# Recurrent attention with two feed-forward stages on one core: the bonus product and its transpose at other places of the unit

## The chip, the cores and the metric

The kernel runs on one core of one Trainium2 chip. The metric is the device time of one execution in microseconds (us); the time before is the median of three runs.

## The reference, cut to what matters

Three stages follow one another. The first is a linear recurrence per batch and head, with a 48 x 48 state, over 768 steps:

```
for t in range(S):
    cur   = outer(u * k[t], v[t])                  # the bonus of the present step
    y[t]  = r[t] @ (state + cur)
    state = w[t][:, None] * state + outer(k[t], v[t])
```

The second is a feed-forward layer on all 3072 tokens, `h = x @ w_in`, `g = h * tanh(softplus(h))`, `x = g @ w_out`. The third routes each token greedily to one of 8 experts of 384 places each, and applies `relu(x @ w1[e]) @ w2[e]`.

## The kernel before, in words

The recurrence is cut into 24 *units*: two groups of 12 consecutive time chunks, each of two sequences' chunk of 64 steps for all 8 heads. The units of a group depend on each other through the state `S`. A unit consists of ten steps, each a small function:

- `att0` (scan of the decays `E`, and `rk` = r * k), `att_inv`, `att1` and `att1b` (scaling of r and k with the decays and their inverses; ScalarE does Ln and Exp, VectorE the rest),
- `bon1` (L423: u times `rk`, the bonus of every step, 16 matmuls into a `Y` buffer, then `bT` by ScalarE) and `bon2` (L429: one transpose of `bT` into another `Y` buffer, then `bt` by ScalarE and L434, which spreads it into the diagonal of `Dt`),
- `att_A` (scores and the state's part, into `A`; then L467 puts the scores into `Dt`), `att_K` (transposes of k into `Y`, moved out as `kn`),
- `att_S` (L494: the new part of the state, into two `Y` buffers; L501 and L503 add and scale on VectorE), and `att4` (L516: the output matmuls; then `xg`, the input of the second stage, by ScalarE and L523; for every second unit six small DMAs move some rows of `xg`, L529).

The pool that `Y` comes from has two buffers, taken in turn by `bon1`, `bon2`, `att_K` and twice by `att_S`. An engine works its instructions off in the order in which they were written.

The second stage runs along with the recurrence. Its tokens are in 12 groups of 256 (two units each); a group has 8 *slots*, a unit therefore four. In each slot stands one chunk of the first product (`mm1`, L611, 18 matmuls into `Hp`, two buffers; ScalarE evicts each twice, as `es` and `hs`) and a share of the second product (`mm2_part`, L659). Per four slots ScalarE does Arctan and two Sin (L621, L631), and Sigmoid, Sin and Ln with Exp each need a table load when their turn comes.

The order of all this is a list of events with a time in slots each, sorted by time; nothing else orders it. The table `CFG` gives the times; a step of unit n stands at 4n - 13 plus the number in `CFG['u']`, which `CFG['un']` may replace for one unit:

```
for nm, o in {**CFG["u"], **CFG["un"].get(n, {})}.items():
    at(4 * n - 13 + o, steps[nm], n)
...
at(t + CFG["mm1"], mm1, t // NS, t % NS)
at(t + CFG["mm2"], mm2, t)
```

`mm1` stands at 0.7 of a slot, `mm2` at 0.275 of the next, `att_S` of a unit at 7.29 and `att4` at 7.3, which is 3.29 and 3.3 in the count of the unit after it. The third stage is not touched.

Of the kernel before, what the change touches and what calls it, by code (L numbers as in the profile page):

```python
# [25 lines left out]
 'ogT': [7.4, 8.45, 9.9, 10.25, 10.95, 11.85, 12.55, 12.75],  # L26
 'ogM': [8.15, 9.35, 10.2, 10.9, 11.35, 11.95, 12.75, 13.95],
 'u': {'att0': -0.5,
       'bon1': 2.57,
       'bon2': 3.5,  # L30
       'r1': 2.7,
       'k1': 3.175,
       'K': 4.91,
# [53 lines left out]
            'k1': 3.2},  # L87
        5: {'y': 7.46,
            'att0': -1.5,
            'bon1': 3.27,  # L90
            'bon2': 5.25,
            'inv': 3.67,
            'r1': 3.7,
            'k1': 4.3,
# [5 lines left out]
            'A1': 6.67,  # L100
            'S': 7.4,
            'att0': 0.0,
            'bon1': 2.87,
            'bon2': 3.85,
            'inv': 3.27,
            'r1': 3.3,
            'k1': 3.9},
        7: {'bon1': 1.37,
            'att0': -0.5,
            'bon2': 4.85,  # L110
            'inv': 2.77,
            'r1': 2.8,
            'k1': 3.4,
# [1 line left out]
            'A1': 5.87,  # L115
            'S': 7.29,
            'y': 7.3},
        20: {'A1': 5.62, 'bon1': 2.57},
        22: {'att0': -0.6, 'bon1': 1.77, 'bon2': 2.45, 'K': 4.46},
        23: {'K': 3.81, 'A1': 6.0, 'y': 7.1}},  # L120
 'rate': [(9, 0), (80, 194), (82, 200), (85, 216), (89, 218), (93, 234), (99, 258)],
 'close_cv': 15.0,
 'close_att': 86.65,
# [1212 lines left out]
```

## Time and profile before

| | |
|---|---|
| median of three runs | 914.36 us (911.02 to 915.53) |
| the profiled execution | 911.8 us |
| its span | 910.1 us |
| TensorE busy | 780.0 us, 86% |
| VectorE busy | 533.2 us, 59% |
| ScalarE busy | 511.5 us, 56% |
| GpSimd busy | 67.0 us, 7% |
| mean granted TensorE clock | 0.933 |

The times of the profile are those of one execution, counted from the start of its span. An engine's busy time is the time in which it executes instructions; the granted clock is the share of TensorE's full clock. In a timeline a row that ends in brackets tells how long the engine stood idle before it and what released it. PE is TensorE, DVE VectorE, ACT ScalarE.

### The profile page before, as it was taken

The page shows a single profiled execution, that of the slowest core. Times are in us where ns is not written, and L with a number is a line of the kernel's source. Part 1 is how long each engine was busy: PE and PEld are TensorE (multiplying, and loading weights), DVE is VectorE, ACT ScalarE, POOL GpSimd, SP SyncE. Part 2 cuts the span into 40 slices and gives each one's busy share as a digit, 9 for nine tenths or more (in the row PEclk, how much of TensorE's full clock was granted, in tenths as well). Part 3 has the DMA queues.
Part 4 walks back from the last instruction along what each step waited for, and adds up shares of the span by engine and source line. Part 5 has one row for each costly group of instructions (what it writes and reads, how often), then busy time and mean ns, then how long its engine had stood idle before and what let it go on. Part 6 is the DMA issues. An engine that isn't in the chain of part 4 may idle for free. (4 is left out here: it accounts for less than half of the span.)

```text
span 910.1 us, 20168 instructions
## 1 busy us (share of the span) xinstructions
PE 780.0 (86%) x8819; PEld 530.5 (58%) x8819; DVE 533.2 (59%) x933; ACT 511.5 (56%) x728; POOL 67.0 (7%) x104
## 2 busy tenths in 40 slices
PE   6874879788897888888879799999987999999997
PEld 3553656566675555556557577655545655555564
DVE  6699856756556555666555633467774455555420
ACT  3357979876776666666676757711002445445421
POOL 2000000000000000000000000100002122223311
PEclk9796999998999889988889999999996999999999
DMA  7950503211212212212202000040042455544300
GB/s 274 268 148 5 174 10 68 54 40 45 49 38 48 49 39 44 47 34 52 45 10 49 15 10 14 15 160 19 19 157 55 165 183 183 182 166 152 117 27 26
DMA packets 22220, 74.12 MB, mean 81 GB/s; under 512 B 4496, under 2 KB 13072, under 8 KB 20080
## 3 DMA queue, kind: packets, MB, share of 16 engines
q1 hardware_dynamic: 19056, 63.35, 23.9%
q0 software_dynamic: 3072, 9.44, 3.3%
q8 instruction: 71, 1.16, 0.6%
q14 instruction: 21, 0.17, 0.1%
HBM read 62.15 MB, written 9.44 MB: 79 GB/s over the span
## 5 line engine op out<-in xcount | busy, mean ns | idle before, releaser
L611 PE MATMUL Hp<-xg,wi 128*128 128x256 f16 x1728 | 228.3, 291 | 7.7 <-DMA xg<-xg 5.4
L659 PE MATMUL X<-wo,g 128*128 128x392 f16 (+1 forms) x1152 | 222.3, 338 | 0.0
L611 PEld LDWEIGHTS <-wi 128*128 128x128 f16 x1728 | 177.1, 105 | 45.2 <-issue 5.2
L659 PEld LDWEIGHTS <-g 128*128 128x128 f16 x1152 | 111.8, 101 | 68.6 <-issue 9.1
L614 ACT ACTIVATE es<-Hp 128x512 f32<-128x512 f32 x96 | 57.5, 598 | 126.9 <-PE Hp L611 126.7
L632 DVE TENSOR_TENSOR hs<-hs,es 128x1024 f32<-128x1024 f32 x48 | 57.7, 1224 | 83.9 <-ACT es L631 83.9
L1181 PE MATMUL Hp<-xe,a 128*128 128x384 f16 (+1 forms) x612 | 100.8, 316 | 6.4 <-DVE hT L1186 5.2
L1198 PE MATMUL X<-a,hT 128*128 128x384 f16 x576 | 97.2, 326 | 0.0
L1181 PEld LDWEIGHTS <-a 128*128 128x128 f16 x612 | 57.6, 98 | 48.3 <-issue 14.4
L1198 PEld LDWEIGHTS <-hT 128*128 128x128 f16 x576 | 56.4, 98 | 34.8
L645 DVE TENSOR_TENSOR g<-hs,g 128x1024 f16<-128x1024 f32 x48 | 58.9, 1246 | 17.1 <-ACT g L374 16.4
L1186 DVE SCALAR_TENSOR_TENSOR hT<-Hp,hT 128x384 f16<-128x384 f32 x64 | 35.3, 553 | 46.8 <-ACT hT L1185 46.8
L429 PE MATMUL Y<-ident,bT 128*128 128x128 f32 x24 | 9.3, 386 | 61.5 <-DVE S L501 55.4
L1127 DVE SCALAR_TENSOR_TENSOR a<-stg,a 128x1024 f16<-128x1024 f32 (+4 forms) x56 | 59.6, 1066 | 3.2 <-ACT a L1124 2.7
L1201 ACT ACTIVATE or<-X 128x384 f32<-128x384 f32 x24 | 11.8, 490 | 81.0 <-issue 60.7
L1124 ACT ACTIVATE a<-stg 128x1024 f16<-128x1024 f32 (+4 forms) x56 | 51.1, 926 | 7.8 <-DMA stg<-in_w_dram 7.8
L631 ACT ACTIVATE es<-es,right 128x1024 f32<-128x1024 f32 x48 | 54.1, 1143 | 0.3
L374 ACT ACTIVATE hs<-Hp 128x512 f32<-128x512 f32 x91 | 54.1, 595 | 0.0
L1185 ACT ACTIVATE hT<-Hp 128x384 f16<-128x384 f32 x64 | 31.4, 490 | 32.9 <-PE Hp L1181 31.8
L1163 DVE SCALAR_TENSOR_TENSOR xe<-cn,xe 128x384 f16<-128x384 f32 x24 | 13.3, 555 | 61.0 <-ACT xe L1162 60.9
L374 ACT ACTIVATE x1o<-X 128x384 f32<-128x384 f32 x19 | 9.4, 494 | 70.2 <-issue 58.8
L621 ACT ACTIVATE es<-es 128x2048 f32<-128x2048 f32 x24 | 46.0, 1915 | 0.1
(196 smaller groups left out, 962.6 us busy)
## 6 DMA issues: line engine op xcount, KB each, us to landing
stg<-in_w_dram SPq DMA_DIRECT2D x16, 1536.0 KB, 7.4
T<-in_rkw_dram SPq DMA_DIRECT2D x42, 289.5 KB, 4.9
v<-in_v_dram SPq DMA_DIRECT2D x24, 192.0 KB, 3.2
raw<-in_w_out_dram SPq DMA_DIRECT2D x6, 768.0 KB, 4.4
x_dram<-x1o SPq DMA_DIRECT2D x48, 96.0 KB, 2.2
wo<-in_w_in_dram SPq DMA_DIRECT2D x4, 768.0 KB, 9.5
raw<-in_w_in_dram SPq DMA_DIRECT2D x2, 768.0 KB, 8.0
g<-in_w_in_dram SPq DMA_DIRECT2D x2, 768.0 KB, 12.3
```

The costliest lines, as they stand in the source:

```text
L374: nc.scalar.activation(dst, src, AF.Copy, scale=scale)
L611: nc.tensor.matmul(h[:, fi, :], wi[:, a, kk, f * P:(f + 1) * P], xg[g][:, b, kk, :], start=(n == 0), stop=(n == 3 * KD - 1))
L614: nc.scalar.activation(es[g, hf][:, 2 * q:2 * q + 2, :], h, AF.Sigmoid, scale=-1.0 / (SX * SWI))
L621: nc.scalar.activation(e, e, AF.Arctan)
L631: nc.scalar.activation(e, e, AF.Sin, scale=-2.0, bias=right)
L632: nc.vector.tensor_tensor(h, h, e, op=ALU.mult)
L645: (nc.vector if on_v("glo", 2 * H_ + q) else nc.gpsimd).tensor_tensor(gt[:, 1, sl], h, gt[:, 0, sl], op=ALU.subtract)
L659: nc.tensor.matmul(x, gt[:, a, ff, m * P:(m + 1) * P], wo[:, b, f, 0:n], start=(f == 0 and i == 0), stop=(f == NF - 1 and i == 2))
L1124: nc.scalar.activation(dst[:, 0], src, AF.Copy, scale=sc_)
L1127: nc.vector.scalar_tensor_tensor(dst[:, 1], src, sc_, dst[:, 0], op0=ALU.mult, op1=ALU.subtract)
L1181: nc.tensor.matmul(ps[:, cs], a1[:, a, kk, f * P:(f + 1) * P], x[:, b, kk, cs], start=(n == 0), stop=(n == 3 * KD - 1))
L1198: nc.tensor.matmul(ps, h[:, a, f, ms], a2[:, b, f, :], start=(n == 0), stop=(n == 3 * NF2 - 1))
```

## The change

The bonus product `bon1` stands at 1.4 instead of 2.57 slots of its unit, and the transpose `bon2` at 2.4 instead of 3.5; units 5, 6 and 7 get times of their own, the entries of units 20 and 22 for these steps go, and `att_K` of unit 23 gets another time. No instruction is added or removed.

```
@@ -26,8 +26,8 @@
  'u': {'att0': -0.5,
-       'bon1': 2.57,
-       'bon2': 3.5,
+       'bon1': 1.4,
+       'bon2': 2.4,
        'r1': 2.7,
        'k1': 3.175,
        'K': 4.91,
@@ -87,8 +87,8 @@
         5: {'y': 7.46,
             'att0': -1.5,
-            'bon1': 3.27,
-            'bon2': 5.25,
+            'bon1': 2.0,
+            'bon2': 4.6,
             'inv': 3.67,
...
@@ -100,14 +100,14 @@
             'S': 7.4,
             'att0': 0.0,
-            'bon1': 2.87,
-            'bon2': 3.85,
+            'bon1': 1.9,
+            'bon2': 2.9,
             'inv': 3.27,
...
         7: {'bon1': 1.37,
             'att0': -0.5,
-            'bon2': 4.85,
+            'bon2': 2.9,
             'inv': 2.77,
...
@@ -115,9 +115,8 @@
-        20: {'A1': 5.62, 'bon1': 2.57},
-        22: {'att0': -0.6, 'bon1': 1.77, 'bon2': 2.45, 'K': 4.46},
-        23: {'K': 3.81, 'A1': 6.0, 'y': 7.1}},
+        22: {'K': 4.46},
+        23: {'K': 4.3, 'A1': 6.0, 'y': 7.1}},
```

The line numbers of the changed kernel are one lower behind the table. On TensorE, around the state's matmuls of unit 14 (L494), the order before is this, with the transpose of unit 15 (L429) between the output matmuls (L516) and the next chunk of the first product (L611):

```order
L659 LDWEIGHTS g
L659 MATMUL X<-wo,g 128x392
L494 MATMUL Y<-v,kn 64x48 x16
L516 MATMUL A<-Dt,v 48x64 x16
L429 MATMUL Y<-ident,bT 128x128
L611 LDWEIGHTS wi
L611 MATMUL Hp<-xg,wi 128x256
```

In the change the same place reads:

```order
L658 LDWEIGHTS g
L658 MATMUL X<-wo,g 128x392
L493 MATMUL Y<-v,kn 64x48 x16
L515 MATMUL A<-Dt,v 48x64 x16
L610 LDWEIGHTS wi
L610 MATMUL Hp<-xg,wi 128x256
```

The transpose no longer stands between the output matmuls and the next chunk. In the change it stands one slot earlier, ahead of the last chunk in front of the state's matmuls, behind a share of the second product:

```order
L658 LDWEIGHTS g
L658 MATMUL X<-wo,g 128x392
L428 MATMUL Y<-ident,bT 128x128
L610 LDWEIGHTS wi
L610 MATMUL Hp<-xg,wi 128x256
```

That was the place of `bon1` before. The product `bon1` of unit 15 has moved ahead of the scores of unit 14 (L458, L464):

```order
L658 LDWEIGHTS g
L658 MATMUL X<-wo,g 128x392
L422 MATMUL Y<-rk,u_T 32x64 x8
L458 MATMUL A<-T_90 64x64 x16
L464 MATMUL A<-T_90,S_135 64x64 x16
L610 LDWEIGHTS wi
L610 MATMUL Hp<-xg,wi 128x256
```

On ScalarE, in the same unit, the order before has `bT` between the two Sin activations (L631) and `bt` behind the eviction of `xg`:

```order
L374 ACTIVATE hs<-Hp 128x512
L630 ACT_TABLE_LOAD
L631 ACTIVATE es<-es,right 128x1024
L374 ACTIVATE bT<-Y 128x128
L631 ACTIVATE es<-es,right 128x1024
L401 ACT_TABLE_LOAD
L402 ACTIVATE inv<-E_137 128x512
L403 ACTIVATE inv<-inv 128x512
L614 ACT_TABLE_LOAD
L614 ACTIVATE es<-Hp 128x512
L374 ACTIVATE hs<-Hp 128x512
```

In the change `bT` stands behind `kn`, and `bt` ahead of the table load for Sin (L629):

```order
L373 ACTIVATE kn<-Y 128x512
L373 ACTIVATE bT<-Y 128x128
L613 ACTIVATE es<-Hp 128x512
L373 ACTIVATE hs<-Hp 128x512
L373 ACTIVATE bt<-Y 128x8
L629 ACT_TABLE_LOAD
L630 ACTIVATE es<-es,right 128x1024 x2
L400 ACT_TABLE_LOAD
L401 ACTIVATE inv<-E_137 128x512
L402 ACTIVATE inv<-inv 128x512
```

Everything from that table load to the next eviction of `Hp` is now queued behind `bt`.

## Rows read from the trace of the kernel before

**Rows 1.** The page, first part: busy time, share of the span, instructions.

```profile
PE 780.0 (86%) x8819; PEld 530.5 (58%) x8819; DVE 533.2 (59%) x933; ACT 511.5 (56%) x728; POOL 67.0 (7%) x104
```

**Rows 2.** Waits: total, times, longest in us; first whole span, then 182 to 522 us.

```profile
PE Y L429 <- DVE S L501: 55.4, 14, 4.8
...
PE Y L429 <- DVE S L501: 54.6, 13, 4.8
```

**Rows 3.** Windows: length; busy us of PE, PEld, DVE, ACT, POOL; granted clock; DMA share, GB/s.

```profile
181.20:520.70 339.50, 281.11 (x3827) 206.61 (x3827) 199.44 (x291) 234.13 (x312) 1.08 (x1) 0.90 0.19 41
...
248.40:266.00 17.60, 17.60 (x219) 12.79 (x220) 9.87 (x13) 11.04 (x14) 0.00 (x0) 0.90 0.17 35
...
312.50:318.10 5.60, 5.60 (x25) 3.57 (x24) 5.38 (x8) 1.67 (x4) 0.00 (x0) 0.52 0.07 15
...
278.00:285.90 7.90, 7.86 (x128) 5.76 (x127) 2.43 (x2) 6.30 (x8) 0.00 (x0) 1.00 0.42 86
```

**Rows 4.** Timeline of PE, one cycle: start us, length us, what, count, idle before.

```profile
312.26 0.47 PE L429 MATMUL Y<-ident,bT 128*128 128x128 f32 x1 [3.89 <-DVE S L501]
312.52 4.05 PE L611 MATMUL Hp<-xg,wi 128*128 128x256 f16 x18
...
318.13 2.13 PE L611 MATMUL Hp<-xg,wi 128*128 128x256 f16 x18
...
322.12 0.69 PE L459 MATMUL A<-T 48*64 48x64 f32 x32
...
326.77 0.43 PE L423 MATMUL Y<-rk,u_T 128*32 128x64 f32 x16
327.13 2.14 PE L611 MATMUL Hp<-xg,wi 128*128 128x256 f16 x18
```

**Rows 5.** Timeline of PE, two cycles that began without a stop (265 and 497 us).

```profile
269.80 2.12 PE L611 MATMUL Hp<-xg,wi 128*128 128x256 f16 x18 [0.61 <-ACT hs L374]
...
278.04 1.47 PE L611 MATMUL Hp<-xg,wi 128*128 128x256 f16 x12 [2.33 <-DMA xg<-xg]
...
508.39 0.50 PE L611 MATMUL Hp<-xg,wi 128*128 128x256 f16 x3 [1.05 <-DMA xg<-xg]
509.42 1.47 PE L611 MATMUL Hp<-xg,wi 128*128 128x256 f16 x12 [0.52 <-DMA xg<-xg]
```

**Rows 6.** Timeline of ACT, the cycle of rows 4.

```profile
311.09 0.59 ACT L374 ACTIVATE hs<-Hp 128x512 f32<-128x512 f32 x1
...
312.77 0.18 ACT L374 ACTIVATE bt<-Y 128x8 f32<-128x8 f32 x1 [0.60 <-PE Y L429]
...
323.06 0.60 ACT L374 ACTIVATE kn<-Y 128x512 f32<-128x512 f32 x1
325.38 0.60 ACT L614 ACTIVATE es<-Hp 128x512 f32<-128x512 f32 x1 [1.72 <-PE Hp L611]
...
326.49 1.28 ACT L630 ACT_TABLE_LOAD   x1
...
328.84 0.26 ACT L374 ACTIVATE bT<-Y 128x128 f32<-128x128 f32 x1
...
334.54 0.59 ACT L374 ACTIVATE hs<-Hp 128x512 f32<-128x512 f32 x1
```

**Rows 7.** Timeline of DVE, the same cycle.

```profile
313.64 0.68 DVE L434 TENSOR_TENSOR Dt<-diag,bt 128x512 f32<-128x512 f32 x1
...
315.39 0.67 DVE L394 TENSOR_TENSOR rk<-T 128x512 f32<-128x512 f32 x1
```

**Rows 8.** Timeline of ACT, the evictions that open and close the fifteen cycles.

```profile
180.57 0.59 ACT L374 ACTIVATE hs<-Hp 128x512 f32<-128x512 f32 x1
...
520.08 0.59 ACT L374 ACTIVATE hs<-Hp 128x512 f32<-128x512 f32 x1
```

**Rows 9.** Timeline of PE behind the last of them.

```profile
521.25 0.47 PE L429 MATMUL Y<-ident,bT 128*128 128x128 f32 x1 [3.89 <-DVE S L501]
521.52 4.05 PE L611 MATMUL Hp<-xg,wi 128*128 128x256 f16 x18
```

More of the change, by code (lines that the diff above doesn't have):

```diff
@@ L28 @@
  'u': {'att0': -0.5,
-       'bon1': 2.57,
-       'bon2': 3.5,
+       'bon1': 1.4,
+       'bon2': 2.4,
        'r1': 2.7,
@@ L89 @@
             'att0': -1.5,
-            'bon1': 3.27,
-            'bon2': 5.25,
+            'bon1': 2.0,
+            'bon2': 4.6,
             'inv': 3.67,
@@ L102 @@
             'att0': 0.0,
-            'bon1': 2.87,
-            'bon2': 3.85,
+            'bon1': 1.9,
+            'bon2': 2.9,
             'inv': 3.27,
@@ L109 @@
             'att0': -0.5,
-            'bon2': 4.85,
+            'bon2': 2.9,
             'inv': 2.77,
@@ L117 @@
             'y': 7.3},
-        20: {'A1': 5.62, 'bon1': 2.57},
-        22: {'att0': -0.6, 'bon1': 1.77, 'bon2': 2.45, 'K': 4.46},
-        23: {'K': 3.81, 'A1': 6.0, 'y': 7.1}},
+        22: {'K': 4.46},
+        23: {'K': 4.3, 'A1': 6.0, 'y': 7.1}},
  'rate': [(9, 0), (80, 194), (82, 200), (85, 216), (89, 218), (93, 234), (99, 258)],
```

## The prediction

> **What bounds the kernel now.** I read the page first. TensorE is busy for 86% of the span [rows 1], so time comes back only where it waits or runs slowly. Next come the waits. One pair stands out: the transpose of `bon2` waits 55.4 us for the state's additions on VectorE, 14 times, and 54.6 us of that, 13 times, lies between 182 and 522 us [rows 2]. I looked at that stretch with the windows. From 181.2 to 520.7 us TensorE is busy 281.1 of 339.5 us at a granted clock of 0.90 [rows 3].
>
> The timeline shows the mechanism. A unit takes four slots, each a chunk of the first product (18 matmuls into `Hp`) and a piece of the second. I call the four chunks of a unit's period a, b, c, d: a follows the scores of `att_A`, b the old place of `bon1`, c comes after the output matmuls, d just before the transposes of `att_K`. The two `Y` buffers go round, so `bon2` needs the buffer that the first half of the state's sum used. That sum stands on VectorE behind the chain that ScalarE's Exp releases. TensorE, which works in order, stands 3.89 us in front of a 0.47 us transpose, with chunk c and everything else behind it [rows 4]. Then the clock is at half: 312.5 to 318.1 shows a granted 0.52, that is 1.2 GHz, where the stretch after the 2.33 us wait at 278 shows 1.00, 2.4 GHz [rows 3, 5]. Chunk c takes 4.05 us, and chunk d starts at 318.13 [rows 4]; a chunk at the full clock takes 2.12 [rows 5].
>
> A cycle can be cut where nothing is ambiguous: at B, the end of ScalarE's last `hs` eviction of chunk b. In the example B is 311.09 + 0.59 = 311.68, the next 334.54 + 0.59 = 335.13, so the cycle takes 23.45 us [rows 6]. It has three pieces: B to chunk d on TensorE 6.45 us (to 318.13), chunk d to ScalarE's `es` eviction of chunk a 7.25 us (to 325.38), and from there to the next B 9.75 us, through three table loads, Sin, Ln and Exp [rows 4, 6].
>
> **What the change does, costed.**
> 1. *The transpose leaves the burst.* Its buffer is then the one that `kn` frees. `kn` ends on ScalarE at 323.06 + 0.60 = 323.66, 3.1 us before the place (326.77) to which the transpose moves [rows 4, 6], so that wait costs nothing; without that cover it would cost up to 3 us a unit. TensorE goes from the output matmuls straight into chunk c at the full clock. What is late next: chunk d needs the `Hp` buffer of chunk b, free at B. The kernel shows this once, in the only cycle without a state burst: chunk d waited 0.61 us and started when ScalarE's `hs` came free [rows 5]. I put 0.1 us between the two, my choice for the handover. The 6.45 us become 0.1, a gain of 6.35.
> 2. *The product `bon1` moves between chunks d and a.* It is 0.36 us of TensorE (326.77 to 327.13 [rows 4]), which used to stand behind chunk a: 7.25 becomes 7.61. It reads `rk`, written on VectorE at 315.39 + 0.67 = 316.06, that is B + 4.4 with the 0.68 us of `Dt` in front [rows 7]; that `Dt` has moved away, so B + 3.7. TensorE reaches `bon1` at B + 0.1 + 3.99 (318.13 to 322.12 [rows 4]) = B + 4.1. The margin is 0.4 us: nothing in the sum, but something in the range.
> 3. *`bt` now stands ahead of the trig table on ScalarE.* The transpose takes the place where `bon1` was, 326.77, and `bt` started 0.51 us after its transpose and took 0.18 [rows 4, 6]: it would end at 327.46, where the table load started at 326.49 before [rows 6], so the chain begins 0.97 us later. `bT` (0.26 us [rows 6]) leaves the space between the Sins; since the two Sins' issue partly covered it I credit 0.2. The 9.75 us become 10.52. This is the new wait that the change adds, and the whole chain to B is queued behind it.
> 4. *`Dt` on VectorE* (0.68 us [rows 7]) goes from the middle of the burst to the front of the Sin products, where VectorE waits for ScalarE anyway; it costs nothing, and would cost 0.7 if VectorE were full.
> 5. *A transfer loses its cover.* Chunk a of every second unit reads `xg` rows that six small DMAs put in place after the output step. At the old pace they landed in time; in the two cycles in which TensorE did not stop before chunk c, it waited 2.33 us, and 1.05 + 0.52 us, for them [rows 5]. Bounds 0 and 2.4, I take the mean of the two, 1.95 us, in the 8 of 15 cycles that open a group.
> 6. *Edits for single units.* Units 5, 6 and 7: the one wait of theirs that the table knows is 55.4 - 54.6 = 0.8 us [rows 2], which I count as gained; the other moves can cost as much, so bounds are +-2. The `K` of unit 23 does nothing (a last chunk has no state). Unit 20 loses only its own values and unit 22 had nearly the new ones before. SP and GpSimd issue the same rows in the same order; the one thing that GpSimd feeds into the moved steps is `rk` of units 4 and 8, inside the same bounds.
>
> **Sum.** The new cycle is 0.1 + 7.61 + 10.52 = 18.23 us. Fifteen cycles lie between B at 180.57 + 0.59 = 181.16 and B at 520.08 + 0.59 = 520.67 [rows 8], 339.5 us. They become 15 x 18.23 + 8 x 1.95 = 273.5 + 15.6 = 289.1, a gain of 50.4. After the last B one wait (3.89) and one half-clock chunk (4.05 - 2.12) go [rows 5, 9]: 5.8. Item 6 adds 0.8; the cycle ahead of 181.16 already pays items 2 and 3, 0.97 - 0.2 + 0.36 = 1.1. Gain 55.9 us. The profiled execution took 911.8 us, 910.1 of it span, so 855.9; I say 856. The median of the runs shown, 914.4, lies 2.6 above the execution, which the range must hold. Against the waits alone (14 of some 4.2 us, with 1.9 us of half clock each, 85 us) this returns two thirds: the rest is held by ScalarE, whose evictions end at B.
>
> **The rivals.**
> - *TensorE becomes the bound.* The cycle from 248.4 to 266.0 had no wait in it: 17.60 us, all busy [rows 3]. If `bt` and `xg` come in time, 15 x 17.6 = 264.0, a gain of 75.5 + 5.5 = 81: 831 us. For it: that cycle. Against it: item 3 is on the path. Chance 0.10.
> - *The new waits are larger.* `bon1` waits for `rk`, or evictions queue behind `bt`: 1 us more in each cycle, and `xg` at 2.85 instead of 1.95 where a token output's eviction stands ahead of it: 15 + 8 x 0.9 = 22 us back, 878 us. Margins of 0.4 us speak for it. Chance 0.17.
> - *The wait only changes its place.* If the transpose waits for `kn` as long as ScalarE's Arctan runs late, 3 us in 14 cycles, 42 us return: 898 us. The 3.1 us of margin speak against it. Chance 0.03; half of that I give to its taking the whole gain, so that nothing is measured.
> - *Slower: the clock stays at half.* The cycle keeps short stops, 1 to 2 us at chunk d and at chunk a, and if each left TensorE at 1.2 GHz, the 8.64 us from chunk d to the transpose's new place (318.13 to 326.77 [rows 4]) would grow by at most the factor of chunk c, 4.05 / 2.12 = 1.91, so by 7.9 us: a cycle of 26.1. Then 15 x 26.1 + 15.6 = 407 against 339.5, less 5.5: 974 us. It decides from about 3.7 us a cycle on. Against it: after 2.33 us of waiting twelve matmuls took 1.47 us, at a granted 1.00 [rows 3, 5]. Chance 0.04. The Trainium skill speaks for this rival (TensorE: Matmul & The Clock Gate, A second HAM failure mode: psum-queue depth-cycling): there, frequent short idling between groups of matmuls made the clock swing between its levels. By that rule the time would be this rival's; the trace shows the fall only after the long stops.
>
> **How the numbers follow.** The forecast has 0.66, with 856 us. The other cases that are faster by over 0.5% (4.6 us, about what a measurement of this kernel can tell from no change) bring that to 0.93; 0.03 stay within it, for the moved wait and for what I have not seen, 0.04 are slower. The range runs from 836, what is left if `bt` costs nothing (15 x 0.77 = 11.6) and `xg` half (7.8), to 878, where the second rival stands.
>
> **What would show it.** In the new profile the wait of the transpose for the state's additions is gone between 182 and 522 us, the granted clock there is above 0.97, and a unit takes about 18 us, a group's first unit 20. Chunk d waits some 1 us for ScalarE's `hs`; chunk a waits for `xg` once per group; ScalarE waits 0.5 to 1 us in front of `bt`. The stretch after 546 us keeps its length. I am wrong if `bon1` waits for `rk`, if a wait of over 3 us stands anywhere in the cycle, or if the clock in that stretch stays near 0.90.

## The result and the profile after

The changed kernel takes 865.78 us (median of 4 runs, 862.77 to 870.7), the kernel before 914.94 beside it; the ratio is 0.9475 (95% interval 0.942 to 0.9531). The forecast was 856, its range 836 to 878: right in sign and in range, 9.8 us too low, with the mechanism that was forecast but for one term (item 6 below). The profiled execution took 864.1 us, 862.4 of it span; the profiled one before took 911.8, so the gain is 47.7 us between the profiles and 49.2 between the medians, where 55.9 was forecast.

The page's first part and TensorE's waits from 170 to 500 us:

```profile
PE 762.9 (88%) x8819; PEld 523.1 (61%) x8819; DVE 530.4 (62%) x933; ACT 508.6 (59%) x728; POOL 66.9 (8%) x104
...
PE Hp L610 <- DMA xg<-xg: 14.8, 8, 2.9
PE Hp L610 <- ACT hs L373: 14.4, 14, 1.7
PE Y L422 <- DVE rk L393: 2.0, 5, 0.7
```

The 55.4 us of the transpose [rows 2] are gone from the list, and with them 3.9 us more that the list of before puts down to L499 and [rows 2] leave out. About half of that has come back at two other places, both foreseen: chunk a waits for the transfers of `xg`, chunk d for ScalarE's `hs`. TensorE is busy 17.1 us less than before [rows 1] with the same instructions, since fewer of them run at half clock. The windows (columns as in [rows 3]) of the fifteen cycles, of a stretch with nothing disturbed, and of two behind a wait for `xg`:

```profile
188.60:480.50 291.90, 259.64 (x3832) 196.06 (x3832) 196.91 (x291) 231.62 (x312) 1.04 (x1) 0.99 0.22 47
252.00:263.00 11.00, 10.40 (x109) 7.81 (x107) 6.00 (x8) 8.65 (x11) 0.00 (x0) 1.00 0.33 73
345.00:352.00 7.00, 5.14 (x87) 3.35 (x80) 3.92 (x6) 1.95 (x5) 0.00 (x0) 0.82 0.40 89
385.00:395.00 10.00, 7.09 (x101) 4.87 (x99) 5.13 (x8) 1.24 (x4) 0.00 (x0) 0.83 0.57 112
```

TensorE's timeline of one cycle, from B at 301.33 + 0.59 = 301.92 (ScalarE's row below), answers to [rows 4]:

```profile
301.97 2.13 PE L610 MATMUL Hp<-xg,wi 128*128 128x256 f16 x18 [1.18 <-ACT hs L373]
...
305.96 0.43 PE L422 MATMUL Y<-rk,u_T 128*32 128x64 f32 x16
...
307.41 0.96 PE L610 MATMUL Hp<-xg,wi 128*128 128x256 f16 x6
310.43 1.47 PE L610 MATMUL Hp<-xg,wi 128*128 128x256 f16 x12 [2.05 <-DMA xg<-xg]
...
313.23 0.27 PE L428 MATMUL Y<-ident,bT 128*128 128x128 f32 x1
...
317.39 0.63 PE L515 MATMUL A<-Dt,v 64*48 64x64 f32 x32
317.95 2.14 PE L610 MATMUL Hp<-xg,wi 128*128 128x256 f16 x18
```

The transpose (313.23) waits for nothing. Chunk c (317.95) follows the output matmuls at once and takes 2.14 us in place of 4.05. ScalarE in the same cycle, for [rows 6]:

```profile
301.33 0.59 ACT L373 ACTIVATE hs<-Hp 128x512 f32<-128x512 f32 x1
...
311.94 0.60 ACT L613 ACTIVATE es<-Hp 128x512 f32<-128x512 f32 x1 [4.18 <-PE Hp L610]
...
313.54 0.18 ACT L373 ACTIVATE bt<-Y 128x8 f32<-128x8 f32 x1 [0.52 <-PE Y L428]
313.73 1.28 ACT L629 ACT_TABLE_LOAD   x1
...
321.62 0.59 ACT L373 ACTIVATE hs<-Hp 128x512 f32<-128x512 f32 x1
```

`bt` starts 1.60 us behind the start of `es`, and the table load stands behind it. B is 321.62 + 0.59 = 322.21: a cycle of 20.29 us that opens a group.

**Where the time went.** ScalarE's evictions that open and close the fifteen cycles:

```profile
188.00 0.59 ACT L373 ACTIVATE hs<-Hp 128x512 f32<-128x512 f32 x1
...
479.88 0.59 ACT L373 ACTIVATE hs<-Hp 128x512 f32<-128x512 f32 x1
```

The first B of the stretch comes at 188.59 (before 181.16 [rows 8]): 7.4 us are lost ahead of it. The fifteen cycles take 480.47 - 188.59 = 291.9 in place of 339.5 us: 47.6 gained. From the last B to the end of the span it is 862.4 - 480.47 = 381.9 in place of 910.1 - 520.67 = 389.4: 7.5 gained. Net 47.7 us, the difference of the spans.

### The profile page after: what moved, and what is told of

Same layout as the page of the kernel before. It is cut to its first block, busy times and chain, and to the rows that moved or that the text cites. A ratio compares the mean times of both kernels' runs of the same rounds, so it can differ in the third digit from the quotient of the medians.

```text
span 862.4 us, 20166 instructions
## 1 busy us (share of the span) xinstructions
PE 762.9 (88%) x8819; PEld 523.1 (61%) x8819; DVE 530.4 (62%) x933; ACT 508.6 (59%) x728; POOL 66.9 (8%) x104
## 5 line engine op out<-in xcount | busy, mean ns | idle before, releaser
L610 PE MATMUL Hp<-xg,wi 128*128 128x256 f16 x1728 | 214.0, 278 | 34.6 <-DMA xg<-xg 18.4
L658 PE MATMUL X<-wo,g 128*128 128x392 f16 (+1 forms) x1152 | 217.7, 334 | 0.3 <-ACT wT L373 0.3
L610 PEld LDWEIGHTS <-wi 128*128 128x128 f16 x1728 | 167.1, 100 | 69.9 <-issue 26.1
L658 PEld LDWEIGHTS <-g 128*128 128x128 f16 x1152 | 109.5, 99 | 64.9 <-issue 4.5
L631 DVE TENSOR_TENSOR hs<-hs,es 128x1024 f32<-128x1024 f32 x48 | 56.8, 1222 | 58.7 <-ACT es L630 58.6
L1147 POOL DMA_INDIRECT xr<-x_dram,idx x24 | 29.2, 1215 | 114.7 <-DVE idx L1098 106.1
```

The lines of the kernel that those rows point to most:

```text
L610: nc.tensor.matmul(h[:, fi, :], wi[:, a, kk, f * P:(f + 1) * P], xg[g][:, b, kk, :], start=(n == 0), stop=(n == 3 * KD - 1))
L631: nc.vector.tensor_tensor(h, h, e, op=ALU.mult)
L658: nc.tensor.matmul(x, gt[:, a, ff, m * P:(m + 1) * P], wo[:, b, f, 0:n], start=(f == 0 and i == 0), stop=(f == NF - 1 and i == 2))
L1147: nc.gpsimd.indirect_dma_start(out=t, out_offset=None, in_=x1_dram[:, :], in_offset=bass.IndirectOffsetOnAxis(ap=idx[:, e * ME + m:e * ME ...
```

## The experiments

The times, with the ratio to the kernel before:

| run | time, us | ratio (95% interval) |
|---|---|---|
| change | 865.78 | 0.9475 (0.942 to 0.9531) |
| e1 units 5, 6, 7 as before | 859.08 | 0.9387 (0.9363 to 0.941) |
| e2 unit 7 as before | 861.63 | 0.9417 (0.9394 to 0.944) |
| e3 transpose back at 3.5 | 924.64 | 1.0125 (1.0092 to 1.0158) |
| e4 `bt` between the Sins | 853.45 | 0.9325 (0.9287 to 0.9363) |
| e5 product at 2.39 | 876.54 | 0.958 (0.9548 to 0.9612) |
| e6 transfers left out | 843.45 | 0.9231 (0.9203 to 0.9259) |
| e7 = e1 + e4 | 850.18 | 0.9295 (0.9266 to 0.9323) |
| e8 = e7 + transfers first | 843.11 | 0.9222 (0.9197 to 0.9247) |
| e9 = e7 + 7 idle matmuls | 848.51 | 0.9266 (0.925 to 0.9281) |
| e10 = e8 + 4 idle matmuls | 850.46 | 0.9282 (0.9264 to 0.93) |
| e11 = e8 + product at 1.77 | 850.21 | 0.928 (0.9264 to 0.9295) |
| e12 = e8 + that in even units | 839.9 | 0.9178 (0.914 to 0.9216) |

**Which of the two moves carries the gain: e3.**

```
-       'bon2': 2.4,
+       'bon2': 3.5,
```

> The change with the general value of the transpose back at 3.5 and the product left at 1.4. Theory (the place of the transpose is the whole gain): the wait of the transpose for the state's additions returns 13 or 14 times with some 4 us each, chunk c is at half clock again, and the time is 910 to 922, the early loss of some 7 us being still there. Rival (the product's move ahead of the scores gave part of the gain): below 900.

It took 924.64 us, 1.25% slower than before and above the 922 that I expected at most. TensorE at the state burst:

```profile
317.26 0.47 PE L428 MATMUL Y<-ident,bT 128*128 128x128 f32 x1 [4.19 <-DVE S L500]
317.53 4.05 PE L610 MATMUL Hp<-xg,wi 128*128 128x256 f16 x18
```

That is the old wait with its half-clock chunk behind it. The gain hangs on the transpose's move. The product's by itself costs: the fifteen cycles take 350.0 us against 339.5. Of that 3.5 us stand in the last cycle alone (23.06 against 19.55), where the kernel before had an early transpose through unit 22's own entry, which e3 lacks; so at most some 7 us are the product's.

**The price of `bt` ahead of the table load: e4.**

```
-       'bon2': 2.4,
+       'bon2': 2.5,
```

> The change with the transpose at 2.5 instead of 2.4: its place on TensorE stays, but bt and Dt now come behind the first Sin. Theory (bt ahead of the table load delays ScalarE's chain by 0.7 to 0.8 us in each of 15 cycles): a cycle that opens no group takes 17.1 to 17.4 us instead of 17.9, and the time is 853 to 858. Rival (the state's matmuls then wait for bt, or VectorE's Dt delays the second Sin product, and the time comes back there): 865 or more.

It took 853.45 us, 12.3 less than the change. In the profiles the fifteen cycles are 8.9 us shorter, and the first four that open no group 0.63 us each. ScalarE and TensorE there:

```profile
308.35 1.28 ACT L629 ACT_TABLE_LOAD   x1
309.64 1.15 ACT L630 ACTIVATE es<-es,right 128x1024 f32<-128x1024 f32 x1
310.70 0.16 ACT L373 ACTIVATE bt<-Y 128x8 f32<-128x8 f32 x1
...
316.94 2.12 PE L610 MATMUL Hp<-xg,wi 128*128 128x256 f16 x18 [0.55 <-ACT hs L373]
```

The load no longer waits, and chunk d waits 0.55 us in place of 1.18. Item 3 is a real price on the path, and the change need not have paid it.

**The place of the product: e5.**

```
-       'bon1': 1.4,
+       'bon1': 2.39,
```

> The change with the product at 2.39 instead of 1.4: the transpose stays off the burst, but the product now stands right ahead of it on TensorE. Theory (the product had to move too, since bT's eviction stands between the two): the transpose waits some 0.5 to 0.7 us for ScalarE's bT in each unit, bt and ScalarE's chain behind it come about 0.7 us later, a cycle that opens no group takes 18.4 to 18.9 us, and the time is 872 to 880. Rival (only the place of the transpose matters): 863 to 869.

It took 876.54 us, as expected. The transpose now waits for the eviction of its own input (ACT `bT`: 6.0 us in 15 waits). The waits for `xg` are 17.9 us, where the change has 14.8; the faster e1 has 17.5, so these explain nothing by themselves.

**The early units: e1 and e2.** e1 puts the entries of units 5, 6 and 7 back, e2 that of unit 7 alone:

```
-            'bon1': 2.0,
-            'bon2': 4.6,
+            'bon1': 3.27,
+            'bon2': 5.25,
...
-            'bon1': 1.9,
-            'bon2': 2.9,
+            'bon1': 2.87,
+            'bon2': 3.85,
...
-            'bon2': 2.9,
+            'bon2': 4.85,
```

> The change with the entries of units 5, 6 and 7 as they were before; all else as in the change. Theory (these entries cost about 7 us, because the bonus of units 6 and 7 is now evicted late in front of the state's matmuls of units 5 and 6): the last eviction of chunk b ahead of unit 8's period comes at 181 to 183 us instead of 188.6, and the time is 857 to 861. Rival (the early loss comes from the general values of units 4 and 8 or from a late landing of the transfers of xg, whatever these entries are): that mark stays at 187 to 190 us and the time at 864 to 868.

> The change with the entry of unit 7 alone as before. Theory (unit 7's transpose behind the third table load makes the state's matmuls of unit 6 wait 1.87 us for bt, and the half clock behind it costs as much again): the mark of unit 8 moves forward by 3 to 4 us, to about 185, and the time is 861 to 863. Rival (it is the wait for xg at 153 us, which units 5 and 6 cause, that does all the harm): the mark moves by less than 1 us.

e1 takes 6.7 us less than the change, clear of noise; e2 takes 4.2 less, but its interval overlaps the change's. In e1 the first B stands at 181.78, 0.6 behind where it was before, and TensorE waits neither for `xg` nor for `bt` ahead of it. In e2 it came at 183.09, earlier than I expected, but one profile says little here: e3, e6, e4 and e5 share the change's entries for these units, and their first B comes at 182.92, 183.15, 188.28 and 189.23. TensorE in the change, ahead of that B:

```profile
153.75 1.69 PE L610 MATMUL Hp<-xg,wi 128*128 128x256 f16 x12 [2.07 <-DMA xg<-xg]
...
164.69 0.66 PE L493 MATMUL Y<-v,kn 64*64 64x48 f32 x27 [1.87 <-ACT bt L373]
...
166.25 3.24 PE L610 MATMUL Hp<-xg,wi 128*128 128x256 f16 x18
```

ScalarE, which it waits for there:

```profile
161.99 1.28 ACT L400 ACT_TABLE_LOAD   x1
...
164.48 0.16 ACT L373 ACTIVATE bt<-Y 128x8 f32<-128x8 f32 x1
```

`bt` of unit 7 stands behind a whole table load with its Ln and Exp, and the state matmuls of unit 6 on TensorE wait for it; half-clock stretches follow. The profiled e6 has both waits as well (1.70 and 3.25 us), but no half clock: it is the fastest of e6's runs, 838.07 us against 842.42 to 844.86 for the others. The windows over this stretch, first the change's, then e6's, show the granted clocks:

```profile
140.00:160.00 20.00, 17.28 (x243) 12.45 (x242) 11.22 (x17) 16.73 (x24) 1.59 (x1) 0.91 0.12 29
160.00:183.50 23.50, 21.63 (x307) 16.19 (x307) 14.14 (x22) 17.01 (x24) 0.00 (x0) 0.93 0.23 53
```

```profile
140.00:160.00 20.00, 15.90 (x192) 11.73 (x189) 13.13 (x18) 17.32 (x22) 1.58 (x1) 1.00 0.26 56
160.00:183.00 23.00, 21.40 (x343) 16.52 (x344) 15.07 (x23) 18.09 (x26) 0.00 (x0) 1.00 0.24 54
```

At the full clock these entries put the first B 1.4 us later than in e1 (183.15 against 181.78); the other 5.4 us of the change's 188.59 go with the half clock.

**The transfers: e6.**

```
-        if m == MG - 1:
+        if m == MG - 1 and n < 8:
```

> The change without the six small transfers of xg for units 9, 11 and so on to 23: part of xg's rows is then not the reference's, and what follows from it neither. Theory (the wait for these transfers and the half clock that two of them leave are all on the path): a cycle that opens a group falls from 20.6 us to the 18.0 of the others, 7 times 2.4 us, and 1.5 us go behind the last unit: 846 to 850. Rival (the wait hides another, for ScalarE's evictions or for rk): above 858.

Without these transfers some rows of `xg` are never filled. It took 843.45 us, 22.3 less than the change and some 2.5 below the range I expected. The window over its cycles has a granted clock of 1.00, though chunk d's 14 waits of up to 1.6 us for `hs` are still in it:

```profile
190.00:470.00 280.00, 262.41 (x3915) 201.35 (x3916) 197.40 (x293) 236.35 (x317) 1.04 (x1) 1.00 0.22 47
```

Five of the seven opening cycles whose transfers are left out fall below 18 us. So the transfers, with the half clock that their waits bring, hold some 20 us of the changed kernel.

**A better version: e7 and e8.** e7 has the edits of e1 and of e4. e8 adds one line, which for the units that close a group puts the output step just ahead of the next state burst, so that VectorE feeds the transfers first:

```
-        for nm, o in {**CFG["u"], **CFG["un"].get(n, {})}.items():
+        early = {'y': 7.28} if n % 2 and 8 < n < 22 else {}
+        for nm, o in {**CFG["u"], **CFG["un"].get(n, {}), **early}.items():
```

> Both changes that helped together: units 5, 6 and 7 as before, and the transpose at 2.5. Theory (they act at different places, so the gains add): 853.5 less 6.7, 845 to 849. Rival (the early gain or the shorter cycle is eaten by longer waits for xg): 851 to 854.

> As e7, and for units 9, 11 and so on to 21 the output step stands ahead of the state's matmuls, so that VectorE writes xg ahead of the state's additions. Theory (the transfers start 0.6 to 0.7 us earlier and the wait for them shrinks by that, with less half clock behind it): 4 to 8 us under e7. Rival (the later additions make the transposes of k wait for their Y buffer, or rk comes later still): no faster than e7, with a new wait of the transposes for the state's additions.

e7 took 850.18 us, short of its forecast: only 3.3 less than e4, where the same entries gave e1 6.7. From unit 8 on e7 has e4's program, yet its opening cycles take 20.27 us on average in the profile and e4's 19.84. The chunks a behind their waits differ in the clock. Two in e7, one in e4, and two in the change:

```profile
303.06 2.49 PE L610 MATMUL Hp<-xg,wi 128*128 128x256 f16 x12 [1.66 <-DMA xg<-xg]
...
341.36 2.74 PE L610 MATMUL Hp<-xg,wi 128*128 128x256 f16 x12 [2.09 <-DMA xg<-xg]
```

```profile
305.74 1.47 PE L610 MATMUL Hp<-xg,wi 128*128 128x256 f16 x12 [2.18 <-DMA xg<-xg]
```

```profile
272.19 1.47 PE L610 MATMUL Hp<-xg,wi 128*128 128x256 f16 x12 [1.87 <-DMA xg<-xg]
...
348.73 2.09 PE L610 MATMUL Hp<-xg,wi 128*128 128x256 f16 x12 [1.83 <-DMA xg<-xg]
```

Why the clock fell more often in e7 is not shown. e8 took 843.11 us, 7.1 less, as expected: waits for `xg` fall from 15.7 to 9.1 us.

**Does standing idle bring the half clock: e9 and e10.** Matmuls of no use ahead of chunk a in each opening cycle, seven on e7, four on e8:

```
+    for g in range(3, 11):
+        at(8 * g + 0.6, warm, 7)
```

> Units 5 to 7 as before and bt between the two Sins (as e7), and seven matmuls of no use (128x128, 128x256, into a Y buffer) ahead of chunk a in each of the eight cycles that open a group. Theory (the half clock in opening cycles comes from TensorE standing idle while it waits for xg): TensorE now works through about 0.8 us of that wait, opening cycles fall from a mean of about 20.3 us to about 19.2, the granted clock of 190 to 470 is 0.99 or more, the time 840 to 845 us. Rival (the clock falls there whatever TensorE does, or the matmuls only add their own time): 850 us or more, and the clock still at 0.96 or so.

> As e8 (the transfers of odd units ahead of the state burst), and four matmuls of no use ahead of chunk a in each cycle that opens a group. Theory: the waits for xg are short there already, and what is left of the half clock is one cycle in eight (22.51 us); covering it gives up to 3.5 us, the four matmuls cost at most 0.5 us each where the wait is shorter than they are: 838 to 844 us. Rival (they only add): 846 to 849 us.

e9 gave a clock of 0.99 in 190 to 470 (0.96 in e7) and waits for `xg` of 4.1 us in place of 15.7, as the theory says; but the opening cycles fell only from 20.27 to 19.81 us on average, and the time by 1.7 us, between the two expectations and within the spread of e7's runs. The clocks are of one profile each, and e4 had 0.98 there with 16.0 us of these waits. The seven matmuls take 1.69 us themselves, draw a `Y` buffer too, and wait 2.6 us in all for ScalarE to free it. So that idle time brings the half clock is neither shown nor refuted. e10 missed: 850.46, even above the rival's 846 to 849. In e8 most of the wait was gone already, and four matmuls put 0.88 us on TensorE's path in each such cycle.

**The product behind chunk a: e11 and e12.** e11 sets 1.77 for all units, e12 for five even units whose cycles open no group:

```
-       'bon1': 1.4,
+       'bon1': 1.77,
```

```
-        early = {'y': 7.28} if n % 2 and 8 < n < 22 else {}
+        early = {'y': 7.28} if n % 2 and 8 < n < 22 else ({'bon1': 1.77} if not n % 2 and 8 < n < 20 else {})
```

> As e8, with the bonus product behind chunk a (its default of 1.77 slots) in place of between d and a. Theory (the product between d and a costs its own 0.43 us on TensorE's path and exposes rk in 8 cycles, 3.5 us): chunk a starts about 0.4 us earlier in each of 15 cycles and the waits for rk are gone, while bT's 0.2 us stays on ScalarE: 837 to 842 us. Rival (chunk a is then only earlier to wait for ScalarE, or bT comes too late for the transpose): 843 us or more.

> As e8, with the bonus product behind chunk a for units 10, 12, 14, 16 and 18 alone, whose cycles wait for no transfer; the odd units keep it ahead of chunk a. Theory (e11 lost in the opening cycles alone, where the product and its wait for rk cover part of the transfer of xg; its other cycles were shorter): these five cycles take 84.3 us in place of e8's 86.1, as they did in e11, the opening ones stay at e8's 19 us, and the time is 840.5 to 842.5 us. Rival (the product behind chunk a costs in itself, by bT ahead of ScalarE's table load, and e11's loss has nothing to do with the transfers): 845 us or more.

e11 missed: 850.21. Chunk a of an opening cycle in it:

```profile
303.87 2.72 PE L610 MATMUL Hp<-xg,wi 128*128 128x256 f16 x12 [2.46 <-DMA xg<-xg]
```

Its cycles that open no group are shorter, 84.3 us for five against 86.1 in e8, but the opening ones rise from 19.03 to 20.35 us on average: without the product in front TensorE reaches the transfer earlier, waits and drops to half clock. e12 tests that reading. It took 839.9 us, 0.6 below what I expected: the five cycles take 83.7 us, the opening ones 18.94 on average. The product behind chunk a is cheaper, except where it stands in front of a wait. e12 is the fastest of all, below both kernels.

One opening cycle, the eleventh of the fifteen, stays at 22.8 us in e12 and took 23.1 in the change. What SyncE issues there in e12:

```profile
358.70 1.10 SPq L674 DMA_DIRECT2D x_dram<-x1o  x2
359.89 1.02 SPq L281 DMA_DIRECT2D T<-in_rkw_dram  x2
361.00 0.38 SPq L292 DMA_DIRECT2D v<-in_v_dram  x1
361.48 3.88 SPq L528 DMA_DIRECT2D xg<-xg  x6
```

DMA issues in that stretch (KB each, median us to landing):

```profile
T<-in_rkw_dram SPq DMA_DIRECT2D x4, 289.5 KB, 4.6
...
xg<-xg SPq DMA_DIRECT2D x6, 16.0 KB, 4.4
```

The six small transfers are issued behind the larger ones and land in 4.4 us, where they take 1.8 in a quiet cycle (286 to 300 us). No run moved those loads, so what the cycle would take without them is open.

## Why the prediction was right, and where it was off

1. *The transpose leaves the burst*: right. From B to chunk d it is 301.97 - 301.92 = 0.05 us, I put 0.1. That the wait goes nowhere else is shown by the waits of the change, and that it was the cause by e3.
2. *The product between d and a*: from chunk d to the eviction `es` of chunk a I had 7.61 us. In the cycle from 283.98, which opens no group, it is 291.64 - 284.03 = 7.61:

```profile
284.03 2.12 PE L610 MATMUL Hp<-xg,wi 128*128 128x256 f16 x18 [1.18 <-ACT hs L373]
...
291.64 0.60 ACT L613 ACTIVATE es<-Hp 128x512 f32<-128x512 f32 x1 [1.83 <-PE Hp L610]
```

   The margin of 0.4 us to `rk` was too thin in five cycles, at 2.0 us in all: `bon1` waiting for `rk` was one of the signs of being wrong that I had named, and it came, small. e12 shows that the place itself costs about 0.5 us where nothing has to be covered.
3. *`bt` ahead of the table load*: right in place, a little smaller. From `es` to the next B I had 10.52; in that cycle it is 301.92 - 291.64 = 10.28. Had it cost nothing, I counted 11.6 us (15 x 0.77) less, towards the lower end of the range; e4 gained 12.3 by the medians and 8.9 in the fifteen cycles of the profiles, so that the match of the medians is partly luck.
4. *`Dt` for nothing*: nothing in the waits speaks against it; no run took it alone.
5. *The transfers*: 18.23 us for a cycle that opens no group met a mean of 18.20, 20.18 for one that opens a group a mean of 20.56. The first agreement is partly luck: six of these seven cycles take 17.86 on average, and the seventh 20.22, with the 48 matmuls of L685 in it, which I had not priced. The 0.38 us more is in the two cycles of 21.83 and 23.14, the two windows with a granted 0.82 and 0.83. The fifteen cycles took 291.9 us, I had 289.1. At the end 7.5 us came back in place of 5.8, 7.4 of them in the one cycle behind the last B (16.12 in place of 23.48 us). From the B after that to the end it is 365.8 us, before 365.9, as expected.
6. *Edits for single units*: this is the term that failed. I counted 0.8 us of gain against 1.1 of cost ahead of the first B, -0.3 in all, with bounds of 2 us on each side, because the table of waits names only 0.8 us there. 7.4 us were lost in the profile. What I priced was the wait that goes; what I did not follow is that in these units ScalarE's order is another, so that `bt` of unit 7 comes behind a Ln and Exp chain, and the state matmuls of unit 6 then wait for `bt`. By e1 the three entries cost 6.7 us, by e7 against e4 3.3; how much of it is paid goes with the clock. Without them the time, 859.1, lies 3 us above the forecast.

The profiles add up: 864.1 is 8.2 us above the 855.9 of the sum, 7.1 of that ahead of the first B (7.4 lost where 0.3 was expected), 2.8 in the fifteen cycles, less 1.7 behind them.

Of the rivals, TensorE as the bound (831) did not come, though e12 goes two thirds of the way from the forecast to it. The larger waits (878) did not either: `bon1` lost 2.0 us, not 15. The moved wait (898) is refuted by the transpose's row. The slower one, a clock that stays at half, came true in single cycles and not in the stretch, whose mean is 0.99. The Trainium skill (TensorE: Matmul & The Clock Gate, A second HAM failure mode: psum-queue depth-cycling) has the clock swing under frequent short idling. This case agrees in part: two windows with waits of 1.83 and 2.91 us for `xg` in them have 0.82 and 0.83, but the stops of up to 1.6 us at chunk d left it at 1.00 throughout e6.

## What to carry to other kernels

On an engine that works in order, a cheap instruction costs what everything behind it waits: where a transpose stands 3.9 us in front of a matmul stream, look at which buffer its pool hands it, and move it to where that buffer is already free. Then price a moved step on the engine that evicts it too, and unit by unit where the order differs: the table of waits shows what you remove, not what you add. Work in front of a transfer that is late anyway is free cover; the same work elsewhere is on the path.

## What the runs showed that I had not expected

Waits of about the same length are followed by either level of the clock. Behind 1.87 and 2.05 us of waiting the change's twelve matmuls took 1.47 us (2.4 GHz throughout), behind 1.83 us 2.09, and e7's behind 1.66 and 2.09 us 2.49 and 2.74, nearer to 1.2 GHz. In e6 no wait at chunk d, of up to 1.6 us, brought a fall. This is why the medians carry the argument for the early units and single profiles don't.
